# Reciprocal loads cut in halves, token loads and a weight conversion moved to earlier blocks, in an attention plus gated feed-forward kernel

## The chip, the cores and the metric

One core of one Trainium2 chip runs the whole kernel in one launch. The metric is the device time of an execution in microseconds, lower is better. The time shown is the median of three executions; a separate execution was recorded by the profiler.

## The reference

Four batches of eight attention heads over 576 tokens of head size 64 are computed, and their output goes through a gated feed-forward layer. Cut to what matters:

```
q_rot, k_rot = rotate(q), rotate(k)
scores = q_rot @ k_rot.T / sqrt(64);  scores -= max(scores)
attn = exp(scores);  attn /= sum(attn) + 1e-9
x = (attn @ v) as 2304 tokens x 512
g = x @ w_gate;  y = (g * sigmoid(g) * (x @ w_val)) @ w_out
```

All data is float32. The kernel splits each operand into a high and a low part and sums three products of parts. The weights are kept as 64-bit numbers in memory and are converted on the chip.

## The kernel before, in words

**Attention.** Two heads make a pair, and there are 16 pairs. The loop of `attn_swiglu` (L1057) runs over 16 pairs times nine blocks; a block holds the score rows of 128 queries. I write [p, b] for block b of pair p. In each block a fixed list of steps runs (`PLAN["order"]`, L31): weight loads, preparation of the next pair's q and k, scores of the next block, transposes of the block before, a part of the attention times v, the exponential, evacuations, the pair's rotary work, the tails, early weight conversion, token loads and folds (`x`), and the last pair's weight conversion (`conv1`). The order on SP (the queue that issues nearly all DMAs) and on POOL is the order of the program. On DVE, ACT and, in the attention, PE a scheduler orders the instructions, but `tc.keep_in_program_order` pins an instruction behind everything that was traced on its engine before it.

**The row maximum.** `peak` (L359) reduces a block's scores on DVE (L367). The exponential on ACT (L385) needs it, the transposes on PE (L428) need the exponential, and DVE and ACT take the transposed blocks out as low and high part (L429, L430).

**q and k of the next pair.** `qk_T` runs in blocks 0, 1 and 2 of the pair before and issues DMAs for three stacks: BD in block 0 (L328, L329), QZ in block 1 (L320, L321), QK in block 2 (L323 to L326). The first scores of the next pair read QK.

**Stores and the sums.** A pair's two output halves are stored in its block 8 (L487) and in block 4 of the next pair (L492, L493). After every fourth pair the reciprocals of the row sums are stored to DRAM (`rstore`). 

**Late tokens and folds.** The feed-forward layer needs normalised tokens. `xload` (L636) loads a chunk of tokens with two DMAs of 192 KB into one of two buffers `Xab`; `xprep` (L644, "fold") adds its two halves on POOL, multiplies by the reciprocals `R` and splits into high and low part (L647, L648, L695, L650, some 3.8 us together). `rload` (L619) loads the reciprocals that belong to a group of four chunks into the one buffer `R`, spread over 64 partitions each (two, four or six DMAs a group). There are 16 chunks in four groups: (0,0), (0,1), (0,2), (1,0). `PLAN["rl"]` gives the block in which a group's reciprocals are issued, `PLAN["xs"]` the block of each chunk's load, `PLAN["xe"]` the block of each fold. Within the step `x` the order is reciprocals, then load, then fold:

```
if [p, b] in P["rl"]: ... moe.rload(s, t)
if [p, b] in P["xs"]: ... pend.append((s, c, t, moe.xload(s, c, t)))
if [p, b] in P["xe"]: moe.xprep(*pend.pop(0), po)
```

**The last pair's weights.** The step `raw1` (L1041) issues the load of a gate weight in [15,0] and of a value weight in [15,1] (L775). `conv1` (L1046) converts the gate weight: nine operations, of which six are on DVE (L754, L756, L757, L758, L759, L760), one on ACT (L741) and two on POOL (L742, L743). `PLAN["c1"]` gives the block of each. The value weight is converted after the attention by the list `first` (L1220), and it shares a work area (`X1`, L774) with the gate weight.

**Feed-forward.** After the attention, `plain` (L1166) computes the first output rows with plain products (`mm`, L790; its results are taken out by L811 on ACT and L812 on DVE), prepares the late tokens (`xlate`, L660) and the sums of token blocks; then `strassen` (L1283) and `Down.run` (L1439) compute the rest with seven block products in place of eight. From `plain` on PE, ACT and DVE run in program order.

Of the kernel before, what the change touches and what calls it, by code (L numbers as in the profile page):

```python
# [23 lines left out]
NCH = DM // 128  # L24
# [13 lines left out]
    vsplit=8,  # L38
    rstore=0,
    cv=[[13, 21, 24, 25, 28, 30, 30, 31, 44, 44, 45], [20, 30, 33, 34, 39, 41, 43, 43, 54, 54, 63]],  # L40
    xs=[[3, 3], [3, 6], [6, 5], [7, 5], [8, 7], [9, 5], [10, 5], [11, 5], [12, 7], [13, 7], [14, 1], [14, 2],
        [14, 8], [15, 0], [15, 2], [15, 4]],
    xe=[[5, 3], [6, 3], [7, 3], [8, 3], [9, 3], [10, 3], [11, 3], [12, 3], [13, 5], [14, 1], [14, 3], [14, 5],
        [15, 1], [15, 3], [15, 5], [15, 7]],
    rl=[[4, 5], [8, 8], [12, 8], [14, 8]],
    c1=[[5, 5, 6, 6, 7, 7, 8, 8, 8], [7]],
)


# [462 lines left out]
class Moe:  # L512
    def __init__(self, tc, keep, pl, yd, rd, hd, od, wg, wv, wo, out):
# [12 lines left out]
        self.ld_p = pool("m_ld", 2)  # L526
        self.R, self.G, self.Oraw = {}, {}, {}
        self.after, self.late = [], []
# [87 lines left out]
    def aux(self):  # L616
        return self.aux_p.tile([128, 512], FP32, name="aux")

    def rload(self, s, t, into=None, only=None):  # L619
        if (s, t) in self.R:  # L620
            R = self.R[s, t]
        else:
            R = self.r_p.tile([128, NCH * BK], FP32, name="R") if into is None else into
            R = R.rearrange("p (c n) -> p c n", c=NCH)
        b0, b1 = 2 * s, 2 * s + 1
        parts = {0: [(b0, 0, 384, 0)], 1: [(b0, 384, 128, 0), (b1, 0, 256, 128)],
                 2: [(b1, 256, 256, 0), (b0, -1, 64, 256), (b1, -1, 64, 320)]}[t]
        for b, col, n, to in parts:
            for h in range(2 if only in (None, b) else 0):
                rb = self.rd[b]  # L630
                off, st = (512 * h + col, 1024) if col >= 0 else (4096 + 64 * h, 128)
                src = bass.AP(tensor=rb.tensor, offset=rb.offset + off, ap=[[0, 64], [st, NCH], [1, n]])
                self.nc.sync.dma_start(out=R[64 * h:64 * h + 64, :, to:to + n], in_=src)
        self.R[s, t] = R

    def xload(self, s, c, t):  # L636
# [297 lines left out]
def attn_swiglu(ctx: ExitStack, tc: tile.TileContext, qk, vr, wg, wv, wo, main, tail, out):  # L934
# [9 lines left out]
    moe = Moe(tc, keep, pl, yd, rd, hd, od, wg, wv, wo, out)  # L944
# [79 lines left out]
    @step  # L1024
    def x(n, p, b):
        if [p, b] in P["rl"]:
            s, t = ((0, 0), (0, 1), (0, 2), (1, 0))[P["rl"].index([p, b])]
            assert {("r", 2 * s)} | ({("r", 1)} if t else set()) <= at.done
            moe.rload(s, t)
        if [p, b] in P["xs"]:  # L1030
            s, c, t = xq.pop(0)
            assert {8 * s + c} | ({4 + c} if t else set()) <= at.done
            if (s, t, c) == (0, 2, 0):
                assert not any(cvq.values())
                moe.xa[1] = [moe.again(f"xa1{x}", [128, 4, BK], F32R, f"xa1{x}") for x in "hl"]
            pend.append((s, c, t, moe.xload(s, c, t)))
        if [p, b] in P["xe"]:
            moe.xprep(*pend.pop(0), po)
# [12 lines left out]
    P, cvq, cv1 = PLAN, {}, {}  # L1051
# [5 lines left out]
    for n in range(NB):  # L1057
        p, b = divmod(n, 9)
# [451 lines left out]
```

## Time and profile before

| what | value |
|---|---|
| median of 3 runs | 700.64 us (699.32 to 702.16) |
| profiled execution | 700.53 us, its span 698.8 us |
| busy in the span | PE 97%, DVE 83%, POOL 67%, ACT 61% |
| mean granted TensorE clock | 0.998 |

The span runs from the first to the last instruction of the profiled execution; its own time is 1.7 us longer. PE is TensorE's matmuls, PEld its weight loads, DVE VectorE, ACT ScalarE, POOL GpSimd, SP SyncE, which issues DMAs. A name with a q (SPq) is an instruction of a queue. In a timeline a row has start, duration, engine, line, operation, output and inputs, count, and in brackets how long the engine had been idle and what released it. A granted clock of 1.00 is 2.4 GHz, 0.50 is 1.2 GHz.

### The profile page before, as it was taken

What the parts mean: (1) busy time and instruction counts of PE and PEld (TensorE: products, weight loads), DVE (VectorE), ACT (ScalarE), POOL (GpSimd) and SP (SyncE); (2) the same over time, 40 slices, a digit from 0 to 9 for tenths busy, and PEclk for the clock granted to TensorE, in tenths of its full rate; (3) what the DMA queues carried; (4) which work ended last, traced back from release to release, by engine and by line L of the source; (5) the groups of instructions that cost most, each with busy time, mean ns of one, the idle gap of its engine ahead of it and who ended that gap; (6) DMA issues with size and microseconds to landing.
All of it is one profiled execution on the core that took longest, in us unless ns stands there. A gap on an engine that the chain in (4) does not pass through costs nothing.

```text
span 698.8 us, 12725 instructions
## 1 busy us (share of the span) xinstructions
PE 680.3 (97%) x4414; PEld 666.7 (95%) x4414; DVE 581.8 (83%) x879; ACT 427.0 (61%) x877; POOL 469.8 (67%) x475
## 2 busy tenths in 40 slices
PE   8999999999999998999999999999999999999998
PEld 7999999999999997989999999999999998999997
DVE  6888998888888886689978888989899599877683
ACT  5889989899899886337453543524525275444341
POOL 8997899999999845988889779578794720000000
PEclk9999999999999999999999999999999999999999
DMA  6888887789887887993124427444454797617101
GB/s 200 216 209 211 220 215 192 209 214 228 225 207 214 222 220 168 233 211 137 47 91 151 151 72 242 155 166 143 148 222 174 243 336 249 204 50 249 65 23 68
DMA packets 78784, 125.76 MB, mean 180 GB/s; under 512 B 16880, under 2 KB 55680, under 8 KB 78720
## 3 DMA queue, kind: packets, MB, share of 16 engines
q1 hardware_dynamic: 75248, 118.77, 58.9%
q10 hardware_dynamic: 3472, 6.18, 2.5%
q8 instruction: 35, 0.57, 0.3%
q14 instruction: 29, 0.24, 0.1%
HBM read 66.91 MB, written 33.10 MB: 143 GB/s over the span
## 4 chain that ended last, share of the span: by engine, by line
PE 71%; DMA 11%; DVE 7%; ACT 3%; POOL 3%; issue 3%; SPq 2%; ACTq 0%; DVEq 0%; POOLq 0%
PE ch L845 31%; PE ch L1475 17%; PE sc L352 7%; PE pv L468 7%; PE tr L428 5%; DMA QK<-N 2%; DMA X<-in_qk_dram 2%; PE ch L797 2%; PE tr L289 1%; DMA raw<-in_moe_w_gate_dram 1%; DMA T2h<-yd 1%; POOL t L205 1%; POOL rot L206 1%; DMA rd<-rr 1%; DMA VR<-in_vr_dram 1%
## 5 line engine op out<-in xcount | busy, mean ns | idle before, releaser
L367 DVE TENSOR_REDUCE nmt<-sc 128x1 f32<-128x576 f32 x144 | 108.3, 752 | 23.4 <-PE sc L352 23.1
L385 ACT ACTIVATE E<-sc,nmt 128x576 f32<-128x576 f32 x128 | 97.5, 762 | 10.3 <-DVE nmt L367 10.2
L428 PE MATMUL tr<-ident,E 128*128 128x128 f32 x512 | 77.3, 274 | 3.8 <-ACT E L385 3.4
L428 PEld LDWEIGHTS tr<-ident,E 128*128 128x128 f32 x512 | 60.8, 140 | 6.1 <-ACT E L385 3.6
L1475 PE MATMUL ch<-dW,dO 128*128 128x384 f32 x216 | 63.9, 337 | 0.7 <-DVE dW L1423 0.7
L352 PE MATMUL sc<-QK 128*128 128x288 f32 x240 | 59.4, 329 | 3.7 <-DMA QK<-N 1.6
L205 POOL TENSOR_TENSOR t<-X,tab 128x256 f32<-128x256 f32 (+2 forms) x94 | 54.3, 599 | 11.8 <-DMA X<-in_qk_dram 8.4
L430 DVE TENSOR_TENSOR ET2l<-tr,ET2h 128x512 fp32r<-128x512 f32 x80 | 53.6, 682 | 3.2 <-ACT ET2h L429 2.9
L429 ACT CAST ET2h<-tr 128x512 fp32r<-128x512 f32 x80 | 47.0, 589 | 8.8 <-PE tr L428 7.9
L352 PE MATMUL sc<-N,QZ 128*128 128x288 f32 x240 | 51.4, 296 | 0.1
L698 POOL TENSOR_TENSOR W<-WF,W 128x1024 fp32r<-128x1024 f32 x20 | 48.1, 2408 | 3.6 <-ACT W L698 3.3
L207 POOL TENSOR_TENSOR rot<-rot,t 128x512 f32<-128x512 f32 (+2 forms) x47 | 47.3, 1007 | 3.7
L206 POOL TENSOR_TENSOR rot<-X,tab 128x512 f32<-128x512 f32 (+2 forms) x47 | 47.1, 1002 | 0.0
L430 DVE TENSOR_TENSOR ET1l<-tr,ET1h 128x512 fp32r<-128x512 f32 x64 | 42.8, 684 | 4.2 <-ACT ET1h L429 4.0
L1475 PE MATMUL ch<-dH,dO 128*128 128x384 f32 x156 | 45.4, 337 | 0.0
L845 PE MATMUL ch<-T1h,W 128*128 128x384 f32 x160 | 44.0, 336 | 0.7 <-DVE sg L820 0.7
L845 PE MATMUL ch<-T2h,W 128*128 128x384 f32 x160 | 44.2, 337 | 0.0
L845 PE MATMUL ch<-T0h,W 128*128 128x384 f32 x160 | 44.2, 337 | 0.0
L352 PEld LDWEIGHTS sc<-QK 128*128 128x128 f32 x240 | 36.7, 190 | 7.1 <-ACT E L385 2.7
L468 PE MATMUL pv<-ET2h,VS 128*128 128x320 f32 x128 | 41.0, 330 | 0.1
L1475 PEld LDWEIGHTS ch<-dW,dO 128*128 128x128 f32 x216 | 39.7, 188 | 1.3 <-DVE dW L1423 1.3
L429 ACT CAST ET1h<-tr 128x512 fp32r<-128x512 f32 x64 | 37.7, 612 | 3.9 <-PE tr L428 3.7
(349 smaller groups left out, 2304.1 us busy)
## 6 DMA issues: line engine op xcount, KB each, us to landing
QK<-N SPq DMA_DIRECT2D x64, 288.0 KB, 4.8
hd<-sg SPq DMA_DIRECT2D x14, 768.0 KB, 3.4
dB<-hd SPq DMA_DIRECT2D x8, 1152.0 KB, 5.8
X<-in_qk_dram SPq DMA_DIRECT2D x15, 576.0 KB, 7.5
yd<-Y SPq DMA_DIRECT2D x31, 256.0 KB, 5.1
raw<-in_moe_w_gate_dram SPq DMA_DIRECT2D x12, 512.0 KB, 4.6
raw<-in_moe_w_val_dram SPq DMA_DIRECT2D x12, 512.0 KB, 3.0
Xab<-yd SPq DMA_DIRECT2D x32, 192.0 KB, 5.2
```

Source lines behind the costliest of these rows:

```text
L205: e.tensor_tensor(out=sel(t2, u), in0=sel(x, w), in1=tb(Sn, u), op=ALU.mult)
L206: e.tensor_tensor(out=o, in0=x, in1=tb(C, slice(0, D)), op=ALU.mult)
L352: nc.tensor.matmul(ps[:, g, 0:288], l, rr[:, o + g * 288:o + (g + 1) * 288], start=(x == 0), stop=(x == len(terms) - 1))
L367: nc.vector.tensor_reduce(out=nmcol, in_=ps[:, :, 0:288], axis=AX.XY, op=ALU.max, negate=True)
L385: nc.scalar.activation(out=E.rearrange("p (a b) -> p a b", a=2), in_=ps[:, :, 0:288], func=ACTF.Exp, bias=nmcol, scale=1.0, accum_out=self ...
L428: nc.tensor.transpose(ps[:, c], E[:, o + c * 128:o + (c + 1) * 128], self.ident)
L429: nc.scalar.copy(dst[0], src)
L430: nc.vector.tensor_tensor(out=dst[1], in0=src, in1=r32(dst[0]), op=ALU.subtract)
L468: nc.tensor.matmul(st["ps"][:, 0:w], VS[:, sl, :], t, start=(x == 0), stop=(x == last))
L698: return [lambda: self.nc.scalar.copy(h, f), lambda: le.tensor_tensor(out=l, in0=f, in1=r32(h), op=ALU.subtract)]
L845: nc.tensor.matmul(acc, l[:, w, c * 128:(c + 1) * 128], r, start=(n == 0 and k not in ONTO), stop=(n == 5), skip_group_check=True)
L1475: nc.tensor.matmul(ps, l, r[:, f], start=(new and f == 0 and x == 0), stop=(f == NFP - 1 and x == 2), skip_group_check=True)
```

## The change

Reciprocals: the three groups after the first are loaded in two halves, chunks 0 and 1 and chunks 2 and 3, straight into the one tile `R[0,0]`, each half after the folds that read its old content. Group (0,1) moves from [8,8] to [8,3] and [9,3], group (0,2) from [12,8] to [11,3] and [13,3], group (1,0) from [14,8] to [14,4] and [15,0]. Token loads, counted from 0: number 9 moves from [13,7] to [13,5], 10 from [14,1] to [14,0], 11 from [14,2] to [14,1], 12 from [14,8] to [14,5], 13 from [15,0] to [14,8]. The folds stay in their blocks. The gate weight's nine conversion steps move from blocks 5 to 8 of the last pair to blocks 4 to 6. The step that issues the weights is not in the diff.

```diff
-    xs=[[3, 3], [3, 6], [6, 5], [7, 5], [8, 7], [9, 5], [10, 5], [11, 5], [12, 7], [13, 7], [14, 1], [14, 2],
-        [14, 8], [15, 0], [15, 2], [15, 4]],
+    xs=[[3, 3], [3, 6], [6, 5], [7, 5], [8, 7], [9, 5], [10, 5], [11, 5], [12, 7], [13, 5], [14, 0], [14, 1],
+        [14, 5], [14, 8], [15, 2], [15, 4]],
...
-    rl=[[4, 5], [8, 8], [12, 8], [14, 8]],
-    c1=[[5, 5, 6, 6, 7, 7, 8, 8, 8], [7]],
+    rl=[[4, 5], [8, 3], [9, 3], [11, 3], [13, 3], [14, 4], [15, 0]],
+    c1=[[4, 4, 5, 5, 6, 6, 6, 6, 6], [7]],
...
-    def rload(self, s, t, into=None, only=None):
+    def rload(self, s, t, into=None, only=None, c0=0, c1=4):
         if (s, t) in self.R:
             R = self.R[s, t]
+        elif c1 - c0 < 4:
+            R = self.R[0, 0]
...
-                src = bass.AP(tensor=rb.tensor, offset=rb.offset + off, ap=[[0, 64], [st, NCH], [1, n]])
-                self.nc.sync.dma_start(out=R[64 * h:64 * h + 64, :, to:to + n], in_=src)
+                src = bass.AP(tensor=rb.tensor, offset=rb.offset + off + c0 * st, ap=[[0, 64], [st, c1 - c0], [1, n]])
+                self.nc.sync.dma_start(out=R[64 * h:64 * h + 64, c0:c1, to:to + n], in_=src)
...
         if [p, b] in P["rl"]:
-            s, t = ((0, 0), (0, 1), (0, 2), (1, 0))[P["rl"].index([p, b])]
+            s, t, c0, c1 = ((0, 0, 0, 4), (0, 1, 0, 2), (0, 1, 2, 4), (0, 2, 0, 2), (0, 2, 2, 4), (1, 0, 0, 2),
+                            (1, 0, 2, 4))[P["rl"].index([p, b])]
...
-            moe.rload(s, t)
+            moe.rload(s, t, c0=c0, c1=c1)
```

## Rows read from the trace of the kernel before

**Rows 1.** The page, part 1: busy time, share of the span, instructions.

```profile
PE 680.3 (97%) x4414; PEld 666.7 (95%) x4414; DVE 581.8 (83%) x879; ACT 427.0 (61%) x877; POOL 469.8 (67%) x475
```

**Rows 2.** Timeline of PE, 160 to 350 us, rows after pauses over 0.3.

```profile
176.42 0.50 PE L352 MATMUL sc<-QK 128*128 128x288 f32 x2 [0.93 <-DMA QK<-N]
...
242.67 0.49 PE L352 MATMUL sc<-QK 128*128 128x288 f32 x2 [0.50 <-DMA QK<-N]
245.77 0.50 PE L352 MATMUL sc<-QK 128*128 128x288 f32 x2 [0.51 <-ACT Y L473]
...
279.73 0.76 PE L428 MATMUL tr<-ident,E 128*128 128x128 f32 x4 [3.35 <-ACT E L385]
...
305.31 0.62 PE L797 MATMUL ch<-xa,w1h 128*128 128x384 f32 x2 [0.81 <-DVE Xab L812]
...
318.01 0.63 PE L797 MATMUL ch<-xm,w0h 128*128 128x384 f32 x2 [1.19 <-ACT sv L811]
346.45 0.44 PE L845 MATMUL ch<-T1h,W 128*128 128x384 f32 x1 [0.74 <-DVE sg L820]
```

**Rows 3.** Windows: stretch, length, busy time (count) per engine, clock, DMA share, GB/s.

```profile
262.00:267.00 5.00, 5.00 (x39) 4.82 (x39) 4.19 (x7) 3.77 (x11) 3.67 (x5) 1.00 0.24 71
267.00:278.00 11.00, 9.38 (x75) 9.04 (x73) 5.67 (x10) 6.91 (x17) 4.81 (x6) 1.00 1.02 230
280.10:283.60 3.50, 3.50 (x14) 3.50 (x13) 3.50 (x5) 1.93 (x8) 3.13 (x5) 0.51 0.74 206
304.50:346.00 41.50, 38.93 (x217) 37.65 (x216) 38.23 (x60) 24.44 (x43) 37.72 (x27) 1.00 0.49 132
```

**Rows 4.** The chain of work that ended last, from 267 us: start, length, what.

```profile
267.86 9.64 DMA raw<-in_moe_w_gate_dram
```

**Rows 5.** Timeline of DVE, pair 15 and the second weight's first operation.

```profile
272.57 0.42 DVE L444 TENSOR_TENSOR TK1l<-tr,TK1h 128x256 fp32r<-128x256 f32 x1
272.90 0.68 DVE L430 TENSOR_TENSOR ET2l<-tr,ET2h 128x512 fp32r<-128x512 f32 x1
277.71 0.43 DVE L754 TENSOR_SCALAR raw<-raw 128x512 uint32<-128x512 uint32 x1 [4.13 <-DMA Xab<-yd]
278.06 0.75 DVE L367 TENSOR_REDUCE nmt<-sc 128x1 f32<-128x576 f32 x1
...
294.02 2.05 DVE L754 TENSOR_SCALAR raw<-raw 128x512 uint32<-128x512 uint32 x1 [5.36 <-POOL w0l L743]
```

**Rows 6.** Timeline of SP, DMA issues of pairs 12 to 15.

```profile
229.42 3.88 SPq L633 DMA_DIRECT2D R<-rd  x6
...
244.37 1.25 SPq L640 DMA_DIRECT2D Xab<-yd  x2
...
251.12 1.28 SPq L640 DMA_DIRECT2D Xab<-yd  x2
252.49 0.61 SPq L323 DMA_DIRECT2D QK<-N  x1
...
265.21 1.24 SPq L633 DMA_DIRECT2D R<-rd  x2
```

**Rows 7.** Timeline of POOL, first and last operation of fold 9.

```profile
248.47 1.02 POOL L647 TENSOR_TENSOR Xab<-Xab 128x384 f32<-128x384 f32 x1 [2.65 <-DMA Xab<-yd]
...
251.28 1.00 POOL L650 TENSOR_TENSOR xa1l<-Xab,xa1h 128x384 fp32r<-128x384 f32 x1
```

**Rows 8.** Tile QK, the one DMA issued at 253.2: time to landing.

```profile
DMA to landing us min/median/max: 6.2/6.2/6.2
```

**Rows 9.** Timeline of PE, the first scores of pair 15.

```profile
259.61 0.51 PE L352 MATMUL sc<-QK 128*128 128x288 f32 x2
```

**Rows 10.** Groups of DVE, 277 to 287 us: busy, mean ns, idle before.

```profile
L758 DVE SCALAR_TENSOR_TENSOR raw<-raw 128x512 uint32<-128x512 uint32 x1 | 1.5, 1485 | 0.0
...
L757 DVE TENSOR_SCALAR raw<-raw 128x512 uint32<-128x512 uint32 x1 | 1.0, 1032 | 0.0
L756 DVE TENSOR_SCALAR raw<-raw 128x512 f32<-128x512 f32 x1 | 0.5, 547 | 0.0
```

## The prediction, made before the changed kernel ran

> **What bounds the kernel now.** I began with the page: PE is busy 97% of the span, every other engine much less [rows 1]. So nothing can be won but PE's idle time and time at a lower clock. The second view is PE's timeline, read for the rows with a bracket, from 160 us on, where the change acts: seven pauses over 0.3 us, 0.93, 0.50, 0.51, 3.35, 0.81, 1.19 and 0.74, together 8.0 us [rows 2]. After 346.5 us the products of `strassen` follow each other, and nothing of the change reaches there.
>
> The reader should see three kinds. Those at 176 and 242 us are scores that wait for QK, the stacked q and k of the next pair; the one at 245.8 follows in the same pair. The large one ends at 279.73: a transpose waited for an exponential. Those at 305, 318 and 346 us lie behind work of DVE and ACT after the attention.
>
> For the large one I read DVE's timeline. DVE ended its last work at 273.58 (272.90 plus 0.68) and stood for 4.13 us before L754, the first conversion of the last gate weight; the next row maximum (L367) sits behind it in DVE's queue and started at 278.06, when its scores had long been there [rows 5]. The bracket names a token load, but L754 reads the weight alone, and the chain has the weight's DMA there, 9.64 us from issue to landing [rows 4]; I follow the chain. The windows say why it took so long: in 262 to 267 the DMA engines had a share of 0.24, in 267 to 278 of 1.02 at 230 GB/s [rows 3]. SP's timeline gives the reason: the reciprocals of group (1,0) were issued only at 265.21 [rows 6], since their tile had to be read by fold 11 first, and behind them stood a token load, the weight, another token load and the second weight. By the shapes in the code these are 768, 384, 512, 384 and 512 KB, 2560 KB, and 230 GB/s for 11 us is what it took. After the pause PE ran at a granted clock of 0.51, about the 1.2 GHz level, in the stretch 280.1 to 283.6 [rows 3]: 0.49 x 3.5 = 1.71 us lost.
>
> **The change, part by part.** *Group (0,1), [8,8] to [8,3] and [9,3].* In [8,8] its loads stood just ahead of BD, QZ and QK of the next pair, and QK came late. Now both halves stand behind that pair's QK. The pause of 0.93 goes: -0.93.
>
> *Group (0,2), [12,8] to [11,3] and [13,3].* Six issues kept SP for 3.88 us ahead of QK of pair 14 [rows 6]. The two pauses of 0.50 and 0.51 go: -1.01.
>
> *Twelve more DMAs.* SP pays by the DMA, not by the byte: six loads of 64 to 256 KB took 0.65 each, two of 384 KB 0.62 each [rows 6]. So the halves cost 12 x 0.63 = 7.6 us of SP in all, hidden while SP has waits and PE's operands lie ahead of them. The cover is thin in [13,3]: the six half loads there take SP as long as the six whole ones did in [12,8], and token load 9, which was issued at 244.37 with SP back to back [rows 6], moves up two blocks in the program and hardly at all in time.
>
> *Token loads 9 to 13.* Load 10 passes pair 15's VR and QZ loads on SP. Load 11 passes its four QK loads, and here a wait is added: there are two buffers, load 11 takes that of load 9, and fold 9 stands later in the same block. Fold 9 ended at 252.28, having waited for its load [rows 7]. Behind load 11 on SP stand the four QK loads, of which the first was issued at 252.49 [rows 6]; with load 11 in front (1.28 as in rows 6) it goes out at 253.65, 1.16 later. The second QK load, issued at 253.2, landed 6.2 later, at 259.4, and the first scores of pair 15 began at 259.61 [rows 8, 9]: 0.25 to spare. With 1.01 won by PE in pair 13 and not by this queue, the new pause is 1.16 - 0.25 + 1.01 = 1.92. Bounds: 0 (load 10 crosses a quiet stretch, QK lands faster) to 3.6 (1.92 plus half a clock loss as above). I take +1.92. Loads 12 and 13 pass a store, the reciprocals and the weight; their data now fills 262 to 267.
>
> *The weight.* Its issue step is not in the diff and it stands in [15,0] before and after; what changes is the queue ahead. Fold 11 no longer holds it: it goes out once load 13 has, near 264.6 against 267.86, an estimate from the order on SP. Ahead of it from 262 on lie half a group (384), loads 12 and 13 (384 each), a store (256), then its own 512: 1920 KB at 230 GB/s are 8.3 us, so it lands at 270.4, or at 274.2 if the 896 KB issued behind it mix in. *The conversion* is pinned behind the tails of block 4, which DVE ended at 272.99 [rows 5], 0.59 earlier than now. So DVE waits 0 to 1.2 us. In front of the next maximum then stand L754 (0.43, or 2.05 as for the second weight) and L756 (0.55) and one eviction of 0.68 [rows 5, 10]; the maximum starts near 274.7 with the short one. Before, 1.67 lay between it (278.06) and the transpose (279.73); so the transpose can start at 276.3 to 277.5, where PE is free at 276.4. I take 0.8 left of the pause, without a fall of the clock, as after the 0.81 and 1.19 pauses, whose window has 1.00 [rows 2, 3]: 0.8 - 3.35 - 1.71 = -4.26. Bounds -5.06 and +0.6.
>
> The same operation took 0.43 and 2.05 [rows 5], so something besides its size sets its length. The Trainium skill, "SBUF — State Buffer", section "Who interferes with whom", says that some DVE operations and a GpSimd operation exclude each other for a whole instruction, and the second one stands. By that rule the two conversions could each wait for a fold's operation; with 1.02 each [rows 7] the sum below would be 2.0 higher. I keep the 0.43, measured with this weight in this stage.
>
> *After the attention.* POOL's two last conversion steps stood behind fold 15, and the second weight's L754 waited 5.36 us for them, till 294.02, because of the shared work area [rows 5]. Now they stand ahead of fold 15, and folds 12 to 15 run earlier with their loads. DVE was busy 38.2 of 41.5 us in 304.5 to 346 [rows 3]; started about 9 us earlier where PE is 4 earlier, it is ahead, and the pauses of 0.81, 1.19 and 0.74 (2.74) shrink. Bounds 0 and -2.74; I take -2.3, as the first is pure queueing behind those conversions.
>
> **Sum:** -0.93 - 1.01 + 1.92 - 4.26 - 2.3 = -6.58, from the profiled execution's 700.53 us, which is 0.11 below the median: 693.95, told as **694.0**.
>
> **Rivals.** *The weight still lands late* (0.20). Speaks for it: 1.02 of DMA share, and loads that mix. Landing at 275 to 277, the pause is 2 to 4 us, the clock falls again: 700.53 - 0.02 - 5.06 + 3 + 1.7 - 2 = 698.2. If its queue position gives no earlier landing at all, that part of the change doesn't do what it says, and it is about 700.5.
>
> *The gain is given back* (0.13): DVE's work after the attention is limited by its inputs and not by its start, PE arrives 4 us earlier and finds it unfinished; new pauses in 300 to 346. Against it speaks the 5.36 wait. Time about 700.
>
> *Conversions starve the maxima* (0.09): the pins put the first four steps (0.43 + 0.55 + 1.03 + 1.49 = 3.5 [rows 5, 10]) ahead of block 7's maximum. With an eviction or two it starts at 278, as before, so the 3.35 and 1.71 stay; the second weight's start then moves little, and QK adds 1.92 against the 1.94 won; the last maximum, with two steps more ahead of it, adds some 1.5: 702.0, slower. It decides from the point at which four and not two steps precede that maximum.
>
> **How the numbers follow.** Forecast 0.58, within 691.5 to 697. The rivals have 0.20, 0.13 and 0.09. About 0.5%, 3.5 us, is what a measurement of this kernel can tell from no change, so faster means under 697.1. Faster: nearly all of the forecast and half of the first rival, 0.67. Slower by over 3.5 us needs the third rival and a longer QK pause: 0.05. The rest, 0.28, is the same. If every pause in rows 2 went, with the clock loss, it would be 700.53 - 9.7 = 690.8; I set the low end at 691.5 and the high end at 699.5, which holds the first rival and leaves out the others, about 2 in 10.
>
> **What would show it.** No pause near 176 and 242; a pause before the first scores of pair 15 released by QK, with load 11 issued right after fold 9's last operation; the weight issued near 264 and landed by 274; DVE idle before L754 under 1.5 us; no stretch at 0.5 clock near 280; the second weight's L754 some 9 us earlier and its wait gone. Wrong, if the weight's landing stays near 277, if maxima stand behind conversions, or if pauses after 300 us grow.

## The result and the profile after

The changed kernel takes 693.9 us (median of 5 runs, 692.91 to 695.02) against 700.64 (5 runs, 699.00 to 702.16). The ratio is 0.9907, its 95% interval 0.9884 to 0.993: 6.7 us less, where the forecast was 694.0. The profiled execution took 695.02 us with a span of 693.2; before it was 700.53 and 698.8. The lines behind `rload` moved by two: L754 to L760 are now L756 to L762, L811 and L812 are L813 and L814, L797 is L799, L640 is L642, L775 is L777.

The page's first part (busy time, share of the span, instructions), to be read against [rows 1]:

```profile
PE 677.4 (98%) x4414; PEld 665.0 (96%) x4414; DVE 583.0 (84%) x879; ACT 426.4 (62%) x877; POOL 469.7 (68%) x475
```

PE has the same 4414 instructions, and in the same order, so each can be compared with itself. Its timeline after the change, all rows with a bracket over 0.3 us from 160 to 350 us (start, duration, engine, line, operation, tiles, in the bracket the idle time and its releaser):

```profile
260.20 0.37 PE L352 MATMUL sc<-QK 128*128 128x288 f32 x1 [1.66 <-DMA QK<-N]
...
263.08 0.37 PE L352 MATMUL sc<-QK 128*128 128x288 f32 x1 [0.49 <-DMA QK<-N]
...
312.58 0.44 PE L799 MATMUL ch<-xm,w0h 128*128 128x384 f32 x1 [1.32 <-ACT sv L813]
...
341.06 0.45 PE L847 MATMUL ch<-T1h,W 128*128 128x384 f32 x1 [1.11 <-DVE sg L822]
```

Of the seven pauses of [rows 2] the first five are gone, the last two are there with 1.32 and 1.11, and there are two new ones, both released by QK of pair 15.

The windows (columns as in [rows 3]); the first, second and fourth are the stretches shown there, the third is the one in which the large pause stood, the fifth is the one after the attention:

```profile
262.00:267.00 5.00, 4.51 (x34) 4.17 (x34) 3.77 (x7) 3.85 (x12) 2.10 (x2) 1.00 0.83 225
267.00:278.00 11.00, 11.00 (x89) 10.86 (x89) 9.46 (x17) 8.78 (x24) 7.23 (x8) 1.00 1.05 243
276.10:284.00 7.90, 7.86 (x55) 7.54 (x54) 7.29 (x12) 5.71 (x14) 3.99 (x5) 1.00 1.07 242
280.10:283.60 3.50, 3.46 (x23) 3.17 (x22) 3.44 (x5) 2.25 (x3) 3.25 (x4) 1.00 1.12 216
299.00:340.50 41.50, 39.63 (x227) 38.95 (x225) 37.65 (x59) 24.25 (x43) 38.38 (x27) 1.00 0.50 132
```

The quiet DMA stretch from 262 to 267 is filled, 0.83 where it was 0.24; the stretch behind it is as full as before; the half clock near 280 is gone in this execution. The five executions of the changed kernel had mean granted clocks of 1.000, 1.000, 0.997, 0.998 and 0.998, and only the first has a trace. One stretch of 3.4 us at half the clock, as in before, makes about 0.998 of such a span, so some of the others probably had one somewhere; they were not slower than the first.

SP's timeline (DMA issues), to be read against [rows 6]:

```profile
238.80 5.52 SPq L635 DMA_DIRECT2D R<-rd  x6
...
245.52 1.24 SPq L642 DMA_DIRECT2D Xab<-yd  x2
...
253.45 1.29 SPq L642 DMA_DIRECT2D Xab<-yd  x2
254.83 0.61 SPq L323 DMA_DIRECT2D QK<-N  x1
...
265.01 1.23 SPq L642 DMA_DIRECT2D Xab<-yd  x2
266.33 0.54 SPq L777 DMA_DIRECT2D raw<-in_moe_w_gate_dram  x1
```

POOL's timeline, the last operation of fold 9, against [rows 7]:

```profile
252.41 1.01 POOL L652 TENSOR_TENSOR xa1l<-Xab,xa1h 128x384 fp32r<-128x384 f32 x1
```

The reader sees the new wait: token load 11 goes out at 253.45, right after fold 9 ends at 253.42, and QK stands behind it, 2.34 us later than before.

DVE's timeline, the first operation of either weight and one eviction, against [rows 5]:

```profile
274.09 0.43 DVE L756 TENSOR_SCALAR raw<-raw 128x512 uint32<-128x512 uint32 x1
...
286.63 1.22 DVE L756 TENSOR_SCALAR raw<-raw 128x512 uint32<-128x512 uint32 x1 [1.57 <-POOL w0l L745]
...
298.71 0.55 DVE L814 TENSOR_TENSOR Xab<-ch,Xab 128x384 f32<-128x384 f32 x1
```

The weight was issued only 1.53 earlier (266.33 against 267.86), but its first conversion began at 274.09 without a bracket, so it had landed in at most 7.8 us instead of 9.64 [rows 4]. The second weight began 7.4 earlier, its wait fell from 5.36 to 1.57.

With the same order on PE one can take the start of one and the same matmul in both traces:

| where | before | after | difference | share of the step |
|---|---|---|---|---|
| before group (0,1)'s pause | 162.22 | 163.69 | +1.47 | (first 100 us) |
| behind it | 179.08 | 179.07 | -0.01 | -1.48 |
| before group (0,2)'s pauses | 239.63 | 239.79 | +0.16 | +0.17 |
| behind them | 245.77 | 244.45 | -1.32 | -1.48 |
| pair 15, behind both QK pauses | 261.92 | 263.08 | +1.16 | +2.48 |
| last part of attention times v | 287.02 | 283.38 | -3.64 | -4.80 |
| behind the 0.81 pause | 305.31 | 300.70 | -4.61 | -0.97 |
| behind the 1.19 pause | 318.01 | 312.58 | -5.43 | -0.82 |
| behind the 0.74 pause | 346.45 | 341.06 | -5.39 | +0.04 |

From 162 to 346 us the change wins 6.86 us. The 1.47 at the top arose within the first 100 us, where the two programs are alike, and for it the two recorded executions differ by 5.51 us only. The other kept traces, of kernels that are alike there too, differ from before by -0.3 to +1.8, so I compare them by their **lead**: how much earlier than in the trace of before PE reaches a matmul, with the difference that it had at 162.22 taken off.

### The profile page after: what moved, and what is told of

The parts are those of the page before. It is cut to its first block, busy times and chain, and to the rows that moved or that the text cites. A ratio compares the mean times of both kernels' runs of the same rounds, so it can differ in the third digit from the quotient of the medians.

```text
span 693.2 us, 12733 instructions
## 1 busy us (share of the span) xinstructions
PE 677.4 (98%) x4414; PEld 665.0 (96%) x4414; DVE 583.0 (84%) x879; ACT 426.4 (62%) x877; POOL 469.7 (68%) x475
## 4 chain that ended last, share of the span: by engine, by line
PE 73%; DVE 9%; DMA 9%; issue 3%; SPq 2%; ACT 2%; POOL 1%; ACTq 0%; DVEq 0%
PE ch L847 28%; PE ch L1478 14%; PE pv L468 10%; PE sc L352 10%; PE tr L428 7%; PE tr L289 2%; DMA QK<-N 2%; DVE dB L1416 2%; DMA dO<-od 1%; DMA T2l<-rd 1%; DVE dW L1426 1%; DVE dO L1397 1%; DMA Xab<-yd 1%; PE tr L438 1%; DMA rd<-rr 1%
```

## The experiments

In all of them before ran beside on the same chip. The leads of PE, from the traces as above (negative is earlier), beside the medians:

| kernel | 262 | 287 | 305 | 318 | 346 | median, us |
|---|---|---|---|---|---|---|
| after | -0.3 | -5.1 | -6.1 | -6.9 | -6.9 | 693.9 |
| after, once more | +0.7 | -4.4 | -5.4 | -7.5 | -7.4 | 695.4 |
| e1, conversions alone | +1.6 | +1.1 | +0.1 | -0.4 | -0.3 | 698.74 |
| e2, (1,0) later alone | -0.1 | -5.2 | -0.2 | -0.2 | -0.2 | 700.27 |
| e3, halves alone | -2.7 | -6.5 | -5.4 | -5.4 | -5.4 | 696.38 |
| e4, load 11 back | -1.0 | -5.6 | -6.2 | -6.2 | -6.1 | 693.69 |
| e5, conversions back | +1.1 | -4.1 | -4.9 | -4.9 | -4.9 | 695.44 |
| e6, conversions from block 5 | +1.4 | -3.3 | -4.3 | -6.6 | -6.6 | 694.11 |
| e7, half of (0,2) later | +2.7 | -2.0 | -3.0 | -5.2 | -5.6 | 695.26 |
| e8, (1,0) later and conversions | -0.9 | -6.1 | -3.5 | -3.5 | -3.5 | 698.42 |
| e9, first two groups alone | +0.6 | -0.2 | -0.2 | -0.2 | -0.2 | 699.88 |
| e10, loads 9 to 11 back | -0.3 | -5.1 | -6.0 | -6.9 | -6.8 | 692.46 |
| e11, the same once more | -2.1 | -6.1 | -7.1 | -7.8 | -7.8 | 694.24 |

**Conversions alone** (before, with):

```diff
-    c1=[[5, 5, 6, 6, 7, 7, 8, 8, 8], [7]],
+    c1=[[4, 4, 5, 5, 6, 6, 6, 6, 6], [7]],
```

> The kernel before with the conversion moved to blocks 4 to 6 alone. My theory (the weight's landing sets the large pause, the conversion's place does not): the weight is issued near 268 and lands near 277.5 as before, DVE reaches L754 about 0.6 us earlier and stands 4 to 5 us, PE's pause before the transposes stays at 3.3 to 4.2 us with the 0.5 clock behind it, the two QK pauses near 176 and 242 stay; 699.5 to 702 us. Rival (the earlier conversion is what removed the pause): pause under 1 us, 695 to 697 us.

698.74 us, ratio 0.9973 (0.9958 to 0.9987), a little under the range expected. PE's timeline:

```profile
282.45 0.33 PE L428 MATMUL tr<-ident,E 128*128 128x128 f32 x1 [3.65 <-ACT E L385]
```

The large pause stays: the weight landed at 279.49 and its first conversion began at 279.71, so the size of the pause comes from the landing, not from the blocks of the conversions. The half clock that I expected behind it did not come; its window (columns as in [rows 3]):

```profile
282.00:287.00 5.00, 4.55 (x30) 4.52 (x31) 5.00 (x10) 4.14 (x12) 4.31 (x6) 1.00 0.61 166
```

The median is 0.3% lower. The recorded execution was the slowest of its eight (701.49), so it can't show where these 0.3% are; in it PE gains only after the attention, where the lead goes from +1.1 to -0.4.

**The weight earlier, one number** (before, with group (1,0) whole, behind the weight's step):

```diff
-    rl=[[4, 5], [8, 8], [12, 8], [14, 8]],
+    rl=[[4, 5], [8, 8], [12, 8], [15, 0]],
```

> The kernel before with one number changed: the whole reciprocals of group (1,0) are issued in [15,0], behind the gate weight, and not in [14,8]. My theory (the weight lands late because fold 11 holds the reciprocals and these hold SP): the weight goes out near 263.5, lands near 271 to 274, the pause near 279 falls under 1.2 us and the 0.5 clock goes, while the pauses near 176 and 242 stay; 694.5 to 697 us. Rival (halving and the token loads are needed, or the conversion's place): the pause stays over 2.5 us, 699 to 701 us.

A miss: 700.27 us, ratio 0.9996 (0.9985 to 1.0006). PE's timeline:

```profile
287.53 0.41 PE L468 MATMUL pv<-ET2h,VS 128*128 128x320 f32 x1 [1.66 <-ACT Y L473]
...
301.68 0.44 PE L797 MATMUL ch<-xa,w0h 128*128 128x384 f32 x1 [2.01 <-ACT Xab L811]
```

and its DVE timeline, the second weight's first operation:

```profile
294.36 2.05 DVE L754 TENSOR_SCALAR raw<-raw 128x512 uint32<-128x512 uint32 x1 [6.61 <-POOL w0l L743]
```

The theory of the weight itself holds: the pause near 279 is gone and PE leads by 5.2 at 287. But all of it is given back by 305: folds 14 and 15 run as late as before, POOL's conversion steps stand behind fold 15, the second weight waits 6.61 us for them, and behind the new pauses the clock was at its lower level for 3.4 us. One cost is of this edit's own making: the reciprocals now stand behind the weight, and fold 12 waits for them, as POOL's timeline shows:

```profile
275.32 1.01 POOL L648 TENSOR_TENSOR Xab<-Xab,R 128x384 f32<-128x384 f32 x1 [4.81 <-DMA R<-rd]
```

Moving the weight alone only moves the pause.

**Both of these** (before, with the two edits above):

> The kernel before with its reciprocals of group (1,0) moved whole to [15,0] and the new conversion blocks, loads and the other groups as before. Theory (the gain of the earlier weight is kept only if POOL's conversion steps leave the stretch in which folds 12 to 15 run): the weight goes out near 265, the large pause near 279 is gone, the second weight's first conversion begins near 286 to 288 instead of 294, no pause near 302 released through the conversions; 696 to 698 us. Rival (the folds' loads, not the conversions' place, gave the gain back): folds 14 and 15 run as late as before, pauses of 1.5 us or more near 288 and 302 stay, 699 to 701 us.

698.42 us, ratio 0.9951 (0.9929 to 0.9972), just between the two ranges. PE's timeline:

```profile
286.67 0.41 PE L468 MATMUL pv<-ET2h,VS 128*128 128x320 f32 x1 [1.39 <-ACT Y L473]
...
302.67 0.44 PE L797 MATMUL ch<-xa,w1h 128*128 128x384 f32 x1 [1.79 <-DVE Xab L812]
```

Each side has one half. The second weight began at 288.45, just past the 286 to 288 expected, and PE keeps 3.5 of its 6.1. But the two pauses that the rival named stay, and the clock was at its lower level for 3.4 us behind them. Fold 12 waits 4.28 us for the reciprocals as in e2, and fold 15 ends at 292.3 (291.3 in before, 290.5 in after). So the conversions' place keeps about half of the gain; that the late folds cost the other half fits this trace and e2's, but no run changed the folds alone.

**Halves alone** (after, with loads and conversions of before):

```diff
-    xs=[[3, 3], [3, 6], [6, 5], [7, 5], [8, 7], [9, 5], [10, 5], [11, 5], [12, 7], [13, 5], [14, 0], [14, 1],
-        [14, 5], [14, 8], [15, 2], [15, 4]],
+    xs=[[3, 3], [3, 6], [6, 5], [7, 5], [8, 7], [9, 5], [10, 5], [11, 5], [12, 7], [13, 7], [14, 1], [14, 2],
+        [14, 8], [15, 0], [15, 2], [15, 4]],
...
-    c1=[[4, 4, 5, 5, 6, 6, 6, 6, 6], [7]],
+    c1=[[5, 5, 6, 6, 7, 7, 8, 8, 8], [7]],
```

> The changed kernel with the token loads and the conversion put back where they stood before, so the reciprocals in halves alone. My theory: the QK pauses near 176 and 242 are gone, there is no QK pause near 260 because load 11 stands behind QK again, the weight is no longer held by fold 11 and the large pause is under 1 us; 691.5 to 694 us, not slower than the changed kernel. Rival (the token loads moved up carry the gain): the large pause stays over 2 us, 697 to 700 us.

A miss by 2.4: 696.38 us, ratio 0.9936 (0.9919 to 0.9952). PE's timeline:

```profile
281.69 0.41 PE L468 MATMUL pv<-ET2l,VS 128*128 128x320 f32 x1 [0.97 <-DVE ET2l L430]
...
301.33 0.44 PE L799 MATMUL ch<-xa,w1h 128*128 128x384 f32 x1 [1.58 <-DVE Xab L814]
```

No pause over 0.3 us at QK, the large pause under 1 us as the theory had it, the best lead of all at 287 (-6.5), and 1.1 of it lost at 301, where the second weight began only at 290.04. The halves bring 4.6 us; e4, which differs from it by the loads 9, 10, 12 and 13 and the conversions, brought 7.3 on the same chip, and its lead over e3 arises after the attention.

**The first two groups alone** (before, with groups (0,1) and (0,2) in halves at the new places by the changed code of `rload` and of the step `x`, (1,0) whole at [14,8], loads and conversions of before):

```diff
-    rl=[[4, 5], [8, 8], [12, 8], [14, 8]],
+    rl=[[4, 5], [8, 3], [9, 3], [11, 3], [13, 3], [14, 8]],
```

> The kernel before with only groups (0,1) and (0,2) in halves at the new places; group (1,0) whole at [14,8], loads and conversions as before. Theory (each of those two moves removes a pause of PE and nothing else): no pauses near 176, 242 and 246, the large pause near 279 with its half clock stays or stands 2 us earlier, 698 to 699.5 us. Rival (time won before the late weight is lost again at it, because the pause ends with the weight's landing and not with PE): the two pauses are gone but the large one is longer by as much, 700 to 701 us.

699.88 us, ratio 0.9979 (0.9955 to 1.0004): no difference that this run can tell, as by the rival. PE's timeline:

```profile
259.57 0.37 PE L352 MATMUL sc<-QK 128*128 128x288 f32 x1 [1.96 <-DMA QK<-N]
...
279.74 0.33 PE L428 MATMUL tr<-ident,E 128*128 128x128 f32 x1 [2.00 <-ACT E L385]
```

PE was 2.4 ahead at 245.8 and 0.6 behind at 262: it came early to QK, waited 1.96, and ran at half the clock for 3.4 us from 260.75 on. Time won there would have gone into the pause at 279 in any case, which ends at the same time as before, 279.74 against 279.73. Alone, the two moves bring nothing that this run can tell.

**What makes QK of pair 15 late.** Three edits of the changed kernel, and it itself once more. Load 11 behind QK again:

```diff
-    xs=[[3, 3], [3, 6], [6, 5], [7, 5], [8, 7], [9, 5], [10, 5], [11, 5], [12, 7], [13, 5], [14, 0], [14, 1],
+    xs=[[3, 3], [3, 6], [6, 5], [7, 5], [8, 7], [9, 5], [10, 5], [11, 5], [12, 7], [13, 5], [14, 0], [14, 2],
```

> The changed kernel with token load 11 put back from [14,1] to [14,2], behind pair 15's QK loads. My theory (load 11 waits for fold 9 and holds QK): the first QK load goes out at 252.1 to 253 and not at 254.8, the pauses of 1.66 and 0.49 before pair 15's scores shrink to under 0.6 together, the large pause does not come back; 691.5 to 693 us, 1 to 2 us faster than the changed kernel. Rival (the queue of DMA data and not the order of issue delays QK): the pauses stay over 1.5 us together and the time is within 0.7 us of the changed kernel's.

693.69 us, ratio 0.9903 (0.9881 to 0.9925): the pause before pair 15 is gone, the time is that of after, so the 1 to 2 us did not come. The first QK load went out at 253.80, later than the 252.1 to 253 expected. And the trace does not show the edit alone, since PE had lost time before pair 13:

```profile
226.76 0.37 PE L352 MATMUL sc<-QK 128*128 128x288 f32 x1 [1.55 <-DMA QK<-N]
```

After has no such pause; with it PE comes later to pair 15, and a late QK shows less there.

> The changed kernel unchanged, run beside the next three as their measure. Both theories: 692.9 to 695.0 us, a QK pause of 1.5 to 2.5 us before pair 15's scores, no large pause near 275.

695.4 us, ratio 0.9921 (0.9902 to 0.994), with a pause of 2.89 before pair 15, both a little above what was expected, and none near 312.

The second half of (0,2) behind load 9:

```diff
-    rl=[[4, 5], [8, 3], [9, 3], [11, 3], [13, 3], [14, 4], [15, 0]],
+    rl=[[4, 5], [8, 3], [9, 3], [11, 3], [13, 7], [14, 4], [15, 0]],
```

> The changed kernel with the second half of group (0,2)'s reciprocals moved from [13,3] to [13,7], behind token load 9. My theory (its six issues hold SP for 3.9 us ahead of load 9, so fold 9 ends late, load 11 waits for it and holds pair 15's QK): load 9 goes out near 241 to 243 and not 245.5, fold 9 ends by 250.5, the first QK load goes out before 253.5, and the pauses of 1.66 and 0.49 shrink to under 1.0 together; 0.7 to 2 us faster than the changed kernel. Rival (SP is no bound there, the data in front of QK is): load 9's place changes and the QK pause stays over 1.5 us; within 0.5 us of the changed kernel.

695.26 us, ratio 0.993 (0.9911 to 0.9949). PE's timeline:

```profile
260.46 0.58 PE L352 MATMUL sc<-QK 128*128 128x288 f32 x1 [3.49 <-DMA QK<-N]
```

Its SP timeline, load 9 and the first QK load:

```profile
240.57 1.26 SPq L642 DMA_DIRECT2D Xab<-yd  x2
...
253.14 0.61 SPq L323 DMA_DIRECT2D QK<-N  x1
```

Its window around the end of the pause (columns as in [rows 3]):

```profile
258.90:265.70 6.80, 5.24 (x23) 5.24 (x24) 2.04 (x3) 1.84 (x5) 4.90 (x6) 0.50 0.76 200
```

The theory of the order on SP falls here. Fold 9 ended at 248.68, so load 11 (251.76) had no wait for it, and QK was issued 1.7 earlier than in after. Yet its loads landed 6.1 to 6.5 us later instead of 4.0 to 5.5, and the pause grew. PE itself was 1.5 us earlier in this execution from the first 100 us on, which may be part of the growth. So the pause does not need the wait for fold 9; that the data still in the DMA queues set the landing is the reading that is left, and no run tests it by itself.

Loads 9, 10 and 11 all at their old places:

```diff
-    xs=[[3, 3], [3, 6], [6, 5], [7, 5], [8, 7], [9, 5], [10, 5], [11, 5], [12, 7], [13, 5], [14, 0], [14, 1],
+    xs=[[3, 3], [3, 6], [6, 5], [7, 5], [8, 7], [9, 5], [10, 5], [11, 5], [12, 7], [13, 7], [14, 1], [14, 2],
```

> The changed kernel with token loads 9, 10 and 11 back at their old places and loads 12 and 13 at their new ones. Theory (loads 9 to 11 in front of QK of the last pair make its pause, and the later stages live on loads 12 and 13 and the conversions): the pause before the first scores of the last pair is under 0.5 us, no pause of over 1 us in 270 to 300; 691.5 to 693.5 us. Rival (folds 9 to 11 run later with their loads, and what they hold up, loads 12 and 13 and the folds behind, costs what QK wins): pauses of 1 us or more return in 275 to 305, 694 to 696 us.

> The same kernel as e10_loads_9_11_back, once more. Theory (loads 9 to 11 at their old places shorten the pause before the last pair's scores, so this version beats the changed kernel by 1 us or more): median 692 to 693.3 us, pause before pair 15 under 1 us. Rival (692.46 was the scatter between executions, in which QK of the last pair lands earlier or later): median 693.5 to 695.5 us, the pause 1.5 us or more.

692.46 us with ratio 0.987 (0.9828 to 0.9911), then 694.24 with 0.989 (0.9858 to 0.9922): the second time is in the rival's range, its pause in the theory's. PE's timeline of the first:

```profile
226.06 0.37 PE L352 MATMUL sc<-QK 128*128 128x288 f32 x1 [1.84 <-DMA QK<-N]
...
259.18 0.37 PE L352 MATMUL sc<-QK 128*128 128x288 f32 x1 [0.50 <-DMA QK<-N]
...
310.90 0.44 PE L799 MATMUL ch<-xm,w0h 128*128 128x384 f32 x1 [1.31 <-ACT sv L813]
```

and of the second:

```profile
259.03 0.37 PE L352 MATMUL sc<-QK 128*128 128x288 f32 x1 [0.69 <-ACT ET2h L429]
...
276.54 0.33 PE L428 MATMUL tr<-ident,E 128*128 128x128 f32 x1 [0.85 <-ACT E L385]
```

With load 11 in front of QK the pause was 1.66, 2.89, 2.29, 2.47 and 3.49 in five executions (after, after again, e5, e6, e7); with load 11 behind it 0.50, 0.69 and under 0.15 in four (e10, e11, e3, e4), and 1.96 in e9, where one issue of QZ took SP 3.09 us ahead of QK. In e4 and e10 PE came late by the pause before pair 13, so only e3 and e11 compare at an equal lead: -3.0 behind group (0,2)'s pauses, -2.8 in after. In both the pause is small, so load 11's place in front of QK is the main cause, though not the only one. As a faster version it is not established: all ten runs of e10 and e11 have a median of 693.65, all nine of after 694.4, and their ranges overlap.

**The conversions' blocks.** After, with the old blocks, and with a start in block 5:

```diff
-    c1=[[4, 4, 5, 5, 6, 6, 6, 6, 6], [7]],
+    c1=[[5, 5, 6, 6, 7, 7, 8, 8, 8], [7]],
```

> The changed kernel with the conversion back in blocks 5 to 8. My theory (POOL's two last steps stand behind fold 15 again, so the second weight's first conversion on DVE starts late, at 289 to 292 in place of 286.6, and PE pauses near 300): no large pause near 275, the QK pause before pair 15 stays, pauses of 1 to 2.5 us come back near 282 and 300; 1.0 to 2.5 us slower than the changed kernel. Rival (the conversion's place is worth nothing once the weight lands early): within 0.5 us of the changed kernel.

695.44 us, ratio 0.9927 (0.9906 to 0.9948). The second weight's first conversion began at 290.02, as expected, but the pauses near 282 and 300 did not come. In the trace the lead grows by 0.7 between 287 and 346 where it grows by 1.8 and 3.0 in the two traces of after; the medians, 695.44 beside 695.4 on the same chip, do not show it. Inconclusive by the time.

```diff
-    c1=[[4, 4, 5, 5, 6, 6, 6, 6, 6], [7]],
+    c1=[[5, 5, 6, 6, 6, 6, 6, 6, 6], [7]],
```

> The changed kernel with only the first two conversion steps put back from block 4 to block 5; the last seven stay in block 6, so POOL's order is that of the changed kernel. My theory (POOL's place counts, not DVE's start): within 0.5 us of the changed kernel, no pause over 1 us near 275. Rival (the start in block 4 is what spreads the conversion between the row maxima): a pause of 1 to 2 us near 277 and 1 to 2 us slower than the changed kernel.

694.11 us, ratio 0.9908 (0.9893 to 0.9923), 1.3 below after on the same chip where 0.5 was the bound, with ranges that overlap: not slower, so the start in block 4 is worth nothing that shows. The second weight began at 285.86 here and at 290.02 in e5, so it is the last steps, ahead of fold 15, that set its start. That this is worth time is read from the leads; the medians of e5 and of after do not show it.

## Why the prediction held, and where it did not

*Groups (0,1) and (0,2)*: forecast -0.93 and -1.01, measured -1.48 each by the table of starts. The pauses named went. The sign and the cause were right; the sum of bracketed pauses over 0.3 us was a little short of what PE lost there. Not foreseen was that the first half of (0,2), at [11,3], can make a new pause: in five of the ten traces that have it there PE waited 0.35 to 1.84 for QK of pair 13 (not in after), in none of the four that have the group at [12,8]. What makes it come and go stays open.

*QK of pair 15*: forecast +1.92, measured +2.48 (+3.07 in the other trace of after). In after the mechanism was the one named, load 11 waits for fold 9 and QK stands behind it; but e7 has the pause without that wait, so load 11's place in front of QK is what e3, e7 and e11 support. Two numbers in it were wrong and offset each other. The first issue of QK came 2.34 later, not 1.16: load 9, of which I wrote that it moves "hardly at all in time", went out 1.15 later, because the six half loads ahead of it took SP 5.52 us and not the 3.88 of the six whole ones; fold 9 and load 11 followed. And the landing took 4.0 to 5.5 instead of 6.2. That the two errors offset each other is luck. In e7 the earlier issue came with the longer landing.

*The weight*: forecast -4.26, measured -4.80. The 3.35 pause and the 1.71 of clock both went, and the 0.8 that I left did not come; some 0.3 came back at the last products. The 1.71 belongs to the executions that were recorded and not to the pause: in e1 a pause of 3.65 at the same place had no half clock behind it. Issued at 266.33 and not near 264.6, the weight had still landed by 274.09, at the end of my 270.4 to 274.2. An earlier issue is not what it takes: in e10 the weight went out as late as in before (267.86 there), by SP's timeline

```profile
267.83 0.54 SPq L777 DMA_DIRECT2D raw<-in_moe_w_gate_dram  x1
```

and its first conversion began at 273.17, at most 5.3 us later, where before took 9.64. What the traces have in common is the data in front of it. In the three kernels whose reciprocals of (1,0) go out whole shortly ahead of the weight, with one token load between (before, e1, e9), it landed at 277.35 to 279.49; in all others, e2 with its one number among them, its conversion began at 272.2 to 276.0.

*After the attention*: forecast -2.3, measured -1.75; this term was mis-sized and is the one that failed by its own step. The 0.81 pause went, as queueing behind the second weight, but the 1.19 and 0.74 pauses did not shrink, they became 1.32 and 1.11; the 0.82 in the row of the 1.19 pause comes from shorter delays ahead of it, the largest an idle time of 0.28 at 310.03 in before. "If pauses after 300 us grow" was one of my signs of being wrong. The second weight began 7.4 and not some 9 us earlier, with 1.57 of its wait left. The chain that ended last of the changed kernel shows what stands in front of the pause at 341 (start, length, what):

```profile
285.36 5.52 DMA rd<-rr
...
291.52 5.50 DMA R<-rd
...
299.67 6.87 DMA T2l<-rd
...
309.47 5.08 DMA hd<-Xab
...
341.06 191.47 PE ch L847 x1092
```

By this chain the work begins with the reciprocals of the last pair, and four transfers follow one another up to 314.55, with DVE's and ACT's work behind them up to 341; it starts when the attention ends, whatever was converted earlier. So the rival in which the gain is given back after the attention had its mechanism right for this part. The pause at 312.58 ends before the last of these transfers lands and hangs on something else: its releaser, an eviction on ACT (L813 at 312.03), stood behind ACT's and DVE's work on the late tokens, which had stood behind ACT's casts of a weight, and one of those had waited for POOL, busy without a pause from 279.76 on. No run tests either chain.

*The terms don't add.* The sum forecast was -6.58, PE's lead is -6.86, the medians differ by 6.74. The terms missed by -1.02 (both groups), +0.56 (QK), -0.54 (weight) and +0.55 (after the attention), and +0.17 lay between the groups, so that the total fits to 0.3 is in part luck. Part of this agreement also hides a slack that I had not seen. In the table of leads the kernels with the new conversions and loads differ by 4.8 us at 262 (e7 +2.7, e11 -2.1) and by 2.2 at 346. Those that come early wait near 312 (1.1 to 1.35 in after, e4, e10, e11), those that come late have no pause there (after again, e6, e7). The +1.92 of QK was thus, it seems, largely paid out of a later wait, and taking load 11 back, in e4 and e10, could win little. That the 312 pause is what absorbs it is read from these traces; no run removed it, and in the traces of e4 and e10 the pause before pair 13 also took 1.55 and 1.84.

*Rivals.* The weight landed early, so the first did not occur; the third did not either: the operations ahead of the next maxima were short (0.43 and 0.56) and DVE's waits small. By the rule of the Trainium skill, "SBUF — State Buffer", section "Who interferes with whom", two conversions could each have waited for POOL. I had kept the 0.43, and in after it came. The last pair of runs shows both cases, POOL's timeline of the first (e10):

```profile
273.21 1.26 POOL L650 TENSOR_TENSOR Xab<-Xab,R 128x384 f32<-128x384 f32 x1
```

its DVE timeline:

```profile
273.17 0.43 DVE L756 TENSOR_SCALAR raw<-raw 128x512 uint32<-128x512 uint32 x1 [0.78 <-POOL Xab L649]
```

POOL's timeline of the second execution of the same kernel (e11):

```profile
273.06 1.01 POOL L650 TENSOR_TENSOR Xab<-Xab,R 128x384 f32<-128x384 f32 x1
```

and its DVE timeline:

```profile
273.14 1.22 DVE L756 TENSOR_SCALAR raw<-raw 128x512 uint32<-128x512 uint32 x1 [0.85 <-POOL Xab L649]
```

Whichever began first, by 0.04 or 0.08 us, had its usual length, and the other was longer, POOL's by 0.24, DVE's by 0.79. The section's rule, that the first to issue holds the pair of ports for its whole instruction and the second stands, agrees with this pair. In the second execution PE then paused for 0.85 at 276.54. The 2.05 of the second weight in before [rows 5] fits too: this operation of POOL began 0.07 ahead of it and ended 0.28 before it did:

```profile
293.95 1.84 POOL L704 TENSOR_TENSOR T0l<-xa1h,xa1l 128x768 f32<-128x768 f32 x1
```

## What to carry to other kernels

Removing the largest pause of the engine that bounds the kernel wins only what the next stages can take: give the work behind it (here the folds, POOL's conversion steps and the second weight) the same head start, or it comes back as a new pause. A transfer that waits behind a transfer that waits for an engine is late by that engine, so look for such an issue in the queue before asking for more bandwidth. Look also at what goes out shortly ahead of a transfer: in e10 the weight landed 4 us earlier without an earlier issue, with the reciprocals no longer whole in front of it. With an unchanged order on the bounding engine, compare the starts of the same instruction in two traces; pauses alone leave out what is absorbed later.

## What the runs showed of the hardware

An issue on SP is no fixed cost, as my 0.63 for each DMA had it: six loads of reciprocals took 3.88 us in before and 5.52 in after, and one and the same load of QZ took 0.59 in e3 and 3.09 in e9. With a QK pause PE ran at half the clock for 3.4 us in e5 (pause 2.29), e6 (2.47) and e9 (1.96), for 6.8 us in e7 (3.49), and not at all in after (1.66) and after again (2.89); nor did it behind the 3.65 of e1. I can't say what tells them apart.
